# The second products of a gated layer written as seven products of sums

## The chip, the cores and the metric

The kernel runs on one core of one Trainium2 chip. The time is the device time of one execution in microseconds; each kernel is judged by the median of several executions. A profile is one further execution, recorded by the hardware profiler. The engines are named as in the profile: PE multiplies matrices (PEld is its loading of the stationary operand), DVE is VectorE, ACT is ScalarE, POOL is GpSimd, and SP only issues transfers.

## The reference

Two layers, each an attention part and a gated part, act on 2048 tokens of 448 features, in float32:

```
x = x + attention(layernorm(x), wqkv, wo)      # 16 heads of 28
x = x + gated(layernorm(x))
gated(y): g = y @ w_gate; u = y @ w_up         # 448 -> 1792
          h = sigmoid(g) * u
          return h @ w_down                    # 1792 -> 448
```

The change concerns `h @ w_down`, the second product of the gated part, in both layers.

## The kernel before

**Precision.** Every operand of a product is held as two float16 parts, high and low. A product is three matmuls: high by high, high by low, low by high.

**The gated part.** The tokens go in four blocks (`b`) of 512; the 1792 inner features go in seven pairs (`p`) of two chunks of 128, `p` and `p + 7`. For each block and pair, in this order:

- `gate_and_up` makes 512 tokens by 256 features of both g and u. It already has the form of seven products of sums in the place of eight, with 256 moving columns each: 78 matmuls (L512, in `of_halves`). Partial results leave the PSUM banks `chain` by copies of ACT (L1338) and the banks `side` by additions of DVE (L1354, L1361). ACT takes the sigmoid (L1365), DVE multiplies (L1368), and the result h, in two tiles `one` and `two`, is split by `split` into high (ACT, L205) and low (DVE, L206).
- `down` (L1295) multiplies h by its rows of `w_down`. It is called one pair late: the products of pair `p` stand on PE behind `gate_and_up` of pair `p + 1`. It is 24 matmuls with 448 moving columns (L1307 to L1309), adding up over the seven pairs of a block in four banks. At the block's end DVE adds the four banks to the residual `x` (L1312).

Between the pairs a list `steps` is worked off: the normalisation, the transfer out and back that turns it, and the sums and splits of the next block's operands (`half_steps`), on DVE, ACT and POOL.

**Order.** The order is the program's own (`manual_schedule`): each engine takes its instructions in the order written, and waits where an operand or a buffer isn't ready.

**Weights.** They are split once, during the attention of the first layer, by `Prepare` (DVE sums and splits, POOL's queue for its transfers), and lie in DRAM as `gu_parts` and `dn_parts`. In the gated part all of w_down's parts are resident (`dn`, four tiles), and three of the seven pairs of gate and up weights. The other four pairs share two places: `WeightsGated.used` (L1264) reloads them on POOL's queue. A pair's gate and up weights are two tiles of 800 KB. All large tiles come from 19 equal slots, handed out in the order in which they came free.

**Attention.** The exponential of the scores is taken by ACT, three units of 128 by 512 in one instruction (L1065); some units are computed by DVE instead (`score_aside`). The digits of the string `FEW` say how many for each head of the first layer.

Of the kernel before, what the change touches and what calls it, by code (L numbers as in the profile page):

```python
# [19 lines left out]
P = 128  # L20
# [20 lines left out]
PS = 2.0 ** -13  # L41
UNIT = 32768.0
# [9 lines left out]
AFTER = (None, 4, 5, None, 1, 2, None)  # L52

# [4 lines left out]
N_SUMS = 25  # L58
SHORT = ((10, 23, 12), (11, 24, 13), (8, 22, 9))
# [4 lines left out]
FEW = "2221121212121233"  # L64
# [41 lines left out]
def interleaved_layers(ctx: ExitStack, tc: tile.TileContext, x_in, wqkv, wo, w_gate, w_up,  # L106
# [143 lines left out]
    class Block:  # L250
# [87 lines left out]
        def steps(self):  # L338
            return [self.norm, self.squares,
                    lambda: (self.store((nc.sync, nc.scalar)), self.gather()),  # L340
                    lambda: None, lambda: None] + (
                        self.half_steps() if self.halves else
                        [lambda: self.ready(0, 1), lambda: self.ready(2, 3)])

# [186 lines left out]
    dn_parts = dpool.tile([4, P, 4, 2, D], F16, name="dn_parts")  # L531
# [323 lines left out]
    class Prepare:  # L855


        def __init__(self):
            nc.vector.memset(sums[:, 3:7], 0.0)
            self.part = cpool.tile([P, 2], F32, name="part", tag="part", bufs=1)  # L860
            self.raws, self.packs = big.ring(2), big.ring(2)
            self.halves = None
            tiles = [("o", 0)] + [("d", j) for j in range(4)] + [("gu", j) for j in range(7)]
            order = [(self.measure, what) for what in tiles] + [
                (self.split, what) for what in tiles[:5] + [(w, p) for p in range(NP)
                                                            for w in ("g", "u")]]
            self.read(*tiles[0])
            self.steps = deque()
            at = 6
            for i, (do, what) in enumerate(order):  # L870
                then = order[i + 1][1] if i + 1 < len(order) else None
                self.steps.append((at, lambda do=do, what=what, then=then:
                                   self.step(do, what, then)))
                at += 4 if do == self.measure else 5 if what[0] in "od" else 10
# [14 lines left out]
        def read(self, kind, j):  # L889
            if kind in "gu" and len(kind) == 1:  # L890
                if self.halves is None:
                    self.halves = big.at(self.raws, "raws", [P, 2, 1024])
                self.next = self.halves[:, (kind == "u") * 1]
            else:
                self.next = big.at(self.raws, "raw", [P, 2048])
            if kind == "o":
                load_rows(self.view(self.next, kind), wo, 0, D, nc.gpsimd)
            elif kind == "gu":
                for i, w in enumerate((w_gate, w_up)):
                    load_rows(self.view(self.next, kind)[:, i], w, j * 2 * P, 2 * P, nc.gpsimd)  # L900
            elif kind in "gu":
# [16 lines left out]
        def view(self, t, kind):  # L918
            if kind == "gu":
                return t.rearrange("p (w s c) -> p w s c", w=2, s=4)  # L920
            if kind in "gu":
                return t[:, 0:1024].rearrange("p (s z n) -> p s z n", s=4, z=2)
            return t[:, 0:4 * D].rearrange("p (s n) -> p s n", s=4)

        def step(self, do, what, then):
# [5 lines left out]
            if what == ("g", 0):  # L931
# [34 lines left out]
        def sizes(self):  # L966
# [4 lines left out]
            both_back(2, 5, 6, 2.0 ** -23)  # L971
# [3 lines left out]
        def split(self, raw, kind, j):  # L975
# [22 lines left out]
            else:  # L998
                n = self.count(j)
                t = big.at(self.packs, "pack", [P, 4, 2, D], F16)  # L1000
                scaled_split(t[:, 0:n, 0], t[:, 0:n, 1], v[:, 0:n], 6, nc.vector)
                self.pack = (dn_parts[j][:, 0:n], t[:, 0:n])
# [19 lines left out]
    def attend(layer, values, heads, last_values, gate, keep):  # L1022
# [133 lines left out]
        def more(g):  # L1156
            if g >= groups:
                return
            for u in main[3 * g:3 * g + 3]:
                if u in side:  # L1160
                    begin.append(side[u])
                if u % (NT * NB) == 8:
# [6 lines left out]
                    elif h == H - 1:  # L1169
                        gate.load_out()  # L1170
                        gate.load_gu(0)
# [33 lines left out]
    def out_project(outs, gate):  # L1205
# [15 lines left out]
        gate.load_gu(1)  # L1221
        gate.load_dn()
        gate.load_gu(2)
# [24 lines left out]
    class WeightsGated:  # L1248
# [3 lines left out]
        def __init__(self):  # L1252
            self.gu, self.dn = {}, []
# [5 lines left out]
        def load_gu(self, p, queue=nc.sync):  # L1259
            self.gu[p] = [big.get("gu", [P, N_SUMS, P], F16) for _ in range(2)]  # L1260
            for m in range(2):
                queue.dma_start(self.gu[p][m], gu_parts[p, m])

        def used(self, b, p):  # L1264

            after = AFTER[p]
            if b == NB - 1 and (after is None or after < p):
                big.put(*self.gu.pop(p))
            elif after is not None:
                big.put(*self.gu.pop(p))  # L1270
                self.load_gu(after, nc.gpsimd)

        def load_dn(self):
            j = len(self.dn)
            n = min(4, NF - 4 * j)
            self.dn.append(big.get("dn", [P, 4, 2, D], F16))
            nc.sync.dma_start(self.dn[-1][:, 0:n], dn_parts[j][:, 0:n])

    def gated(layer, first, wt, before_next):
        last = layer == LAYERS - 1  # L1280
        gu, dn = wt.gu, wt.dn
        wt.load_dn()
        wt.load_gu(3)
        wt.load_dn()
        wt.load_gu(6)
        wt.load_dn()
# [4 lines left out]
        pend = []  # L1291
        accs = {}
        held = {j: min(4, NF - 4 * j) for j in range(4)}

        def down(b, p, a, hl):  # L1295


            begin, end = p == 0 and a == 0, p == NP - 1 and a == 1
            if begin:
                accs[b] = [bank(j, "dnp")[:, 0:D] for j in range(TB)]  # L1300
            for j in range(TB):
                f = p + NP * (j // 2 ^ a)
                dw = dn[f // 4][:, f % 4]
                c = j if a == 0 else (j + 2) % 4
                s = slice(c * P, (c + 1) * P)
                pm = accs[b][j]
                nc.tensor.matmul(pm, hl[:, 0, s], dw[:, 0, :], start=begin, stop=False)  # L1307
                nc.tensor.matmul(pm, hl[:, 0, s], dw[:, 1, :], start=False, stop=False)  # L1308
                nc.tensor.matmul(pm, hl[:, 1, s], dw[:, 0, :], start=False, stop=end)  # L1309
                if end:  # L1310
                    t = b * TB + j
                    nc.vector.scalar_tensor_tensor(x[:, t, :], pm, back[:, 2:3], x[:, t, :],  # L1312
                                                   op0=ALU.mult, op1=ALU.add)
                    if last:
                        nc.sync.dma_start(x_dst[:, t, :], x[:, t, :])
            qrt.put(hl)
            if b == NB - 1 and a == 1:
                for f in (p, p + NP):
                    held[f // 4] -= 1
                    if not held[f // 4]:  # L1320
                        big.put(dn[f // 4])

        def gate_and_up(blk, w):
# [9 lines left out]
            lo, hi = slice(0, W // 2), slice(W // 2, W)  # L1333
# [33 lines left out]
            def times(out, v):  # L1367
                nc.vector.scalar_tensor_tensor(out, v, PS, out, op0=ALU.mult, op1=ALU.mult)  # L1368

            first(0)  # L1370
            first(1)
            apart(0)
            second(0)
            second(1)
            apart(1)
            third(0)
            third(1)
            c11_c22(0)
            c11_c22(1)
            sigmoid(one[0], one[0])  # L1380
# [4 lines left out]
            times(two[0][:, hi], chain[1][:, lo])  # L1385
            c12(0)
# [3 lines left out]
            qrt.put(one[1], two[1])  # L1390
            hls = []
# [6 lines left out]

        for b, p in seq:
            if p == 0:  # L1400
# [3 lines left out]
                elif not last:  # L1404
# [3 lines left out]
                    steps.extend([after[1].norm, after[1].squares, after[1].store,  # L1408
                                  after[1].gather])
            hls = gate_and_up(blks[b], gu[p])  # L1410
            wt.used(b, p)
# [4 lines left out]
            pend = [(b, p, a, hls[a]) for a in range(2)]  # L1416
            for f in (2 * p, 2 * p + 1):
                if 2 <= f:
                    run_fill(steps)
                if b == NB - 1 and not last:  # L1420
                    before_next(f)
        for d in pend:
            down(*d)
        return after if not last else None

# [39 lines left out]
    for layer in range(LAYERS):  # L1465
# [6 lines left out]
        def before_next(f, wq=wq):  # L1472
            if f == 6:
# [31 lines left out]
```

## Time and profile before

| | |
|---|---|
| median of three runs | 1931.62 us (1931.43 to 1933.78) |
| profiled execution | 1932.95 us, span 1930.8 us |
| PE busy in the span | 1915.8 us, 23392 matmuls |
| ACT, DVE, POOL busy | 1314.0, 1248.2, 164.5 us |
| first attention, from 120 us to 573.5 us | ACT busy 447.07 us with L1065 |
| gated part of layer 0, 607 to 976 us | PE busy 368.70 us, DVE 201.83, ACT 150.78 |
| gated part of layer 1, 1561 to 1927 us | PE busy 365.70 us, DVE 183.72, ACT 146.65 |
| granted PE clock | full in every slice |

The matmuls are pipelined: the record of one is longer than its share of the time. What a matmul costs in a stream is read from the distance between the starts of consecutive ones, not from its recorded duration.

### The profile page before, as it was taken

How to read it: one execution, taken by the hardware profiler on the slowest of the kernel's cores; microseconds unless marked ns; L12 is line 12 of the kernel's file. 1: busy time of each engine (PE TensorE's matmuls, PEld its weight loads, DVE VectorE, ACT ScalarE, POOL GpSimd, SP SyncE). 2: the span in 40 equal slices, each digit the busy share in tenths (PEclk: the TensorE clock that was granted, in tenths of full speed). 3: DMA queues.
4: the chain of work that ended last, by engine and by line, in shares of the span. 5: the costliest groups of instructions: out<-in, count | busy, mean ns of one | idle time of the engine just before them, and what ended most of it. 6: DMA issues, size and time to landing. Idle time of an engine off the chain costs nothing. (4 is left out here: it accounts for less than half of the span.)

```text
span 1930.8 us, 53585 instructions
## 1 busy us (share of the span) xinstructions
PE 1915.8 (99%) x23392; PEld 1327.5 (69%) x23392; DVE 1248.2 (65%) x2348; ACT 1314.0 (68%) x1574; POOL 164.5 (9%) x308
## 2 busy tenths in 40 slices
PE   8999999999999999999999999999999999999999
PEld 4455555555566777777744568799898777777776
DVE  6638878778676555555574487787778664655543
ACT  5569999999983344444345799999999544343432
POOL 2013322221001000000000000000000000000000
PEclk9999999999999999999999999999999999999999
DMA  5566664334216313232334321122111243333310
GB/s 172 158 197 176 187 195 129 107 102 113 64 62 242 107 69 108 81 128 79 101 111 131 94 51 47 30 51 51 42 36 65 104 169 117 107 111 97 115 49 20
DMA packets 90533, 201.49 MB, mean 104 GB/s; under 512 B 10830, under 2 KB 58030, under 8 KB 90160
## 3 DMA queue, kind: packets, MB, share of 16 engines
q1 hardware_dynamic: 65680, 111.02, 19.7%
q0 software_dynamic: 17776, 83.51, 13.0%
q8 instruction: 185, 3.03, 0.7%
q10 hardware_dynamic: 6832, 3.44, 0.7%
q14 instruction: 60, 0.49, 0.1%
HBM read 142.61 MB, written 47.98 MB: 99 GB/s over the span
## 5 line engine op out<-in xcount | busy, mean ns | idle before, releaser
L1065 ACT ACTIVATE prob_s<-sc 128x1536 f32<-128x1536 f32 x658 | 890.8, 1490 | 8.6 <-PE sc L1050 6.0
L1101 PE MATMUL acc<-prob_s,val_s 128*32 128x256 f32 (+3 forms) x7732 | 591.6, 383 | 0.0
L1050 PE MATMUL sc<-qp_s 114*32 114x512 f16 x7888 | 575.8, 379 | 0.9 <-ACT prob_s L1065 0.9
L512 PEld LDWEIGHTS <-gu_s 128*128 128x128 f16 x4368 | 427.3, 98 | 60.7 <-issue 1.3
L1050 PEld LDWEIGHTS <-qp_s 114*32 114x32 f16 x8192 | 315.8, 95 | 173.0 <-issue 80.0
L1101 PEld LDWEIGHTS acc<-prob_s,val_s 128*32 128x32 f32 x7732 | 321.5, 110 | 96.2 <-issue 7.0
L1354 DVE TENSOR_TENSOR one_q<-side,one_q 128x512 f32<-128x512 f32 x112 | 71.9, 683 | 298.0 <-PE side L512 298.0
L512 PE MATMUL chain<-xwide_s,gu_s 128*128 128x256 f16 x2016 | 247.5, 273 | 0.6 <-ACT one_q L1338 0.5
L1338 ACT COPY one_q<-chain 128x256 f32<-128x256 f32 x224 | 83.0, 372 | 205.5 <-PE chain L512 201.6
L1081 DVE SCALAR_TENSOR_TENSOR power_q<-power_q,expo_q 128x512 f32<-128x512 f32 x228 | 157.8, 692 | 7.8
L1307 PE MATMUL dnp<-dn_s,hhl_q 128*128 128x448 f16 x448 | 157.9, 352 | 0.0
L1308 PE MATMUL dnp<-dn_s,hhl_q 128*128 128x448 f16 x448 | 157.9, 352 | 0.0
L1309 PE MATMUL dnp<-dn_s,hhl_q 128*128 128x448 f16 x448 | 157.9, 352 | 0.0
L512 PE MATMUL side<-xshort_s,gu_s 128*128 128x256 f16 x1120 | 140.9, 272 | 0.0
L497 PE MATMUL qkp<-xhl_s,wqk_s 128*128 128x512 f16 x616 | 139.8, 383 | 0.4 <-ACT xhl_s L466 0.3
L497 PEld LDWEIGHTS <-wqk_s 128*128 128x128 f16 x616 | 60.6, 99 | 71.5 <-issue 2.7
L1130 DVE STREAM_TRANSPOSE oturned_q<-acc 128x512 f32<-128x512 f32 x32 | 22.9, 716 | 130.9 <-PE acc L1101 130.8
L512 PE MATMUL side<-xwide_s,gu_s 128*128 128x256 f16 x672 | 91.7, 273 | 0.0
L1101 PE MATMUL acc<-power_q,val_s 128*32 128x128 f32 (+3 forms) x284 | 88.6, 394 | 0.0
L1338 ACT COPY two_q<-chain 128x256 f32<-128x256 f32 x112 | 41.7, 372 | 67.4 <-PE chain L512 67.4
L1365 ACT ACTIVATE one_q<-one_q 128x512 f32<-128x512 f32 x56 | 35.3, 630 | 59.5 <-DVE one_q L1354 59.5
L1075 DVE TENSOR_SCALAR expo_q<-aside,base 128x512 f32<-128x512 f32 x76 | 56.8, 748 | 28.7 <-PE aside L1050 28.4
(188 smaller groups left out, 2080.0 us busy)
## 6 DMA issues: line engine op xcount, KB each, us to landing
gu_s<-gu_parts POOLq DMA_DIRECT2D x56, 800.0 KB, 4.9
qp_s<-qk_scr SPq DMA_DIRECT2D x96, 224.0 KB
gu_s<-gu_parts SPq DMA_DIRECT2D x20, 800.0 KB
qk_scr<-qkhl_q SPq DMA_DIRECT2D x56, 256.0 KB
gu_parts<-pack_s POOLq DMA_DIRECT2D x14, 800.0 KB, 3.9
xraw_s<-xt_scr SPq DMA_DIRECT2D x12, 768.0 KB
xt_scr<-xs_s SPq DMA_DIRECT2D x34, 224.0 KB
qp_s<-qk_scr SPq DMA_DIRECT2D x64, 112.0 KB
```

The costliest lines, as they stand in the source:

```text
L497: nc.tensor.matmul(pm, w, x, start=(i == 0), stop=(i == len(terms) - 1))
L512: nc.tensor.matmul(pm, a, x, start=(first and i == 0), stop=(i == len(terms) - 1), skip_group_check=True)
L1050: nc.tensor.matmul(ps[32 * j:32 * j + 32, :], hd.k[:, keys], hd.q[:, qb * W:(qb + 1) * W], start=True, stop=True, tile_position=(0, 32 * j))
L1065: nc.scalar.activation(prob[:, 0:n, :], ps[:, 0:n, :], AF.Exp, scale=exp_scale)
L1075: nc.vector.tensor_scalar(y, ps, base2[:, 0:1], -126.0, op0=ALU.mult, op1=ALU.max)
L1081: nc.vector.scalar_tensor_tensor(p, p, c[k], y, op0=ALU.add, op1=ALU.mult)
L1101: nc.tensor.matmul(acc[qb * VC:(qb + 1) * VC, s], v[:, kc % TB, h, :], probs[c * NB + qb][:, s], start=(kc == 0 and a == 0), stop=(kc == N ...
L1307: nc.tensor.matmul(pm, hl[:, 0, s], dw[:, 0, :], start=begin, stop=False)
L1308: nc.tensor.matmul(pm, hl[:, 0, s], dw[:, 1, :], start=False, stop=False)
L1309: nc.tensor.matmul(pm, hl[:, 1, s], dw[:, 0, :], start=False, stop=end)
L1338: nc.scalar.copy(to, pm)
L1354: nc.vector.tensor_tensor(one[m], side[m], one[m], op=ALU.add)
```

## The change

`w_down` is quartered for each pair: two chunks of features by two halves of 224 columns. h of a block is quartered too: two halves of 256 tokens by the two chunks. The eight products of quarters become seven products of sums (Winograd's form). Each is 256 tokens by 128 features by 224 columns, so six matmuls of 224 moving columns for a pair, 42 for a pair's seven products.

- **Weights.** `Prepare` makes seven steps `w` instead of four `d`: four subtractions of DVE and the high and low parts of seven (eight for the first three pairs) quarters or sums, in `dn_parts` with product as first index.
- **h.** Where `split` cast 512 columns twice and subtracted twice, `Operands` makes four sums of 256 columns on DVE, seven high parts of 256 on ACT and seven low parts of 256 on DVE. They are kept in a `store` of seven slots until the next block.
- **Order on PE.** Product `k` of block `b - 1`, over all its pairs, runs inside pair `p = k` of block `b`, in six places between the groups of `gate_and_up` (`along(0)` to `along(5)`). The first three pairs of block 0 (`USUAL`) keep eight products as 24 matmuls of 448 columns, one pair late as before. The last block's seven products stand by themselves at the end.
- **Sums in PSUM.** Products share banks 0 or 3, 1, and 2; after each product DVE adds a bank (or half of it) to its quarter of `x`: seven additions a block instead of four.
- **Residence.** Gate and up weights are now loaded for every pair, two pairs deep; w_down's parts are loaded product by product, three deep, on POOL's queue. The usual pairs' parts are loaded in `out_project` on SP's.
- **First attention.** `FEW` goes from 28 to 25 units on DVE. Steps of `Prepare` stand closer (7 instead of 10 places for a gate or up step).
- The next block's `steps` run in the places named by `portions`, two in a pair in most pairs.

```diff
-FEW = "2221121212121233"
+FEW = "2221212111111133"
+TAIL = (0, 1, 3, 2, 5, 4, 6)
...
+                s12, s34 = [qrt.get("sums", [P, 2, DN]) for _ in range(2)]
+                b11, b12, b21, b22 = [v[:, z, c:c + DN] for z in (1, 0) for c in (0, DN)]
+                for to, a, b in ((s12[:, 0], b12, b11), (s12[:, 1], b22, s12[:, 0]),
+                                 (s34[:, 0], b22, b12), (s34[:, 1], b21, s12[:, 1])):
+                    nc.vector.tensor_tensor(to, a, b, op=ALU.subtract)
...
+        def used_gu(self):
+            big.put(*self.gu.popleft())
+            if self.pairs:
+                self.load_gu(nc.gpsimd)
+
+        def used_dn(self):
+            big.put(self.dn.popleft())
+            if self.products:
+                self.load_dn(nc.gpsimd)
...
+            def high(self, ks, v):
+                for to, a in places(self.b, self.p, ks, v):
+                    nc.scalar.copy(to[:, :, 0], a)
+
+            def low(self, ks, v):
+                for to, a in places(self.b, self.p, ks, v):
+                    nc.vector.tensor_tensor(to[:, :, 1], a, to[:, :, 0], op=ALU.subtract)
+
+            def early(self):
+
+                self.s12, self.s34 = [qrt.get("hsums", [P, 2, W // 2]) for _ in range(2)]
+                a11, a22, a21 = self.one[:, 0], self.one[:, 1], self.two[:, 0]
+                self.high((0, 6), self.one)
+                for to, a, c, op in ((self.s12[:, 0], a21, a22, ALU.add),
+                                     (self.s12[:, 1], self.s12[:, 0], a11, ALU.subtract),
+                                     (self.s34[:, 0], a11, a21, ALU.subtract)):
+                    nc.vector.tensor_tensor(to, a, c, op=op)
+                self.high((1, 2), self.s12)
+
+            def late(self):
+                nc.vector.tensor_tensor(self.s34[:, 1], self.two[:, 1], self.s12[:, 1],
+                                        op=ALU.subtract)
+
+            def parts(self):
+                self.high((4, 5), self.s34)
+                self.high((3,), self.two[:, 1:2])
+                self.low((0, 6), self.one)
+                self.low((1, 2), self.s12)
+
+            def rest(self):
+                self.low((4, 5), self.s34)
+                self.low((3,), self.two[:, 1:2])
+                qrt.put(*self.tiles, self.s12, self.s34)
...
+        def piece(b, k, p, w, j, i, begin):
+
+            a = place(b, p, k)
+            pm = banks_of[i][:, j * DN:(j + 1) * DN]
+            t = slice(j * P, (j + 1) * P)
+            for n, (x, y) in enumerate(((0, 0), (0, 1), (1, 0))):
+                nc.tensor.matmul(pm, a[:, x, t], w[:, p, y], start=(begin and j == n == 0),
+                                 stop=(n == 2), skip_group_check=True)
...
+            if b > 0:
+                some = [q for q in (0, 1, 6, 2, 3, 4, 5) if q in of_block(b - 1)]
+                for q in some:
+                    i = {0: 0, 1: 1, 6: 2, 2: 3, 3: 4}.get(q, 5)
+                    at[i].append(lambda q=q, begin=(q == some[0]): pieces(
+                        b - 1, p, [q], wt.dn[0], begin))
...
+        b = NB - 1
+        w = list(wt.dn)
+        made.parts()
+        made.rest()
+        finish(*done)
+        for n in range(3):
+            pieces(b, TAIL[n], range(NP - 1), w[n], True)
+        for n in range(3):
+            pieces(b, TAIL[n], [NP - 1], w[n])
+            wt.used_dn()
+            finish(b, TAIL[n])
+        for k in TAIL[3:]:
+            if k == 6:
+                banks_of[0] = bank(0, "dnp")
+                for j in range(2):
+                    for p in range(NP):
+                        piece(b, k, p, wt.dn[0], j, 0, p == 0)
+                    add(b, 0, 0, 0, (j,))
+                    if last:
+                        t = b * TB + j
+                        nc.sync.dma_start(x_dst[:, t, :], x[:, t, :])
...
```

More of the change, by code (lines that the diff above doesn't have):

```diff
@@ L1252, in __init__ @@
         def __init__(self):
[L1253 removed]
+            self.gu, self.dn = deque(), deque()
+            self.pairs = deque(p for b in range(NB) for p in range(NP))
+            self.products = deque(list(range(NP)) * (NB - 1) + list(TAIL))
         def load_out(self):
@@ L1290, in gated, with place, places @@
         steps = deque()
[L1291 to L1298, printed above, removed]
-            if begin:
-                accs[b] = [bank(j, "dnp")[:, 0:D] for j in range(TB)]
+        banks_of = {}
+        def place(b, p, k):
+            return store[p][:, k] if b % 2 == 1 else store[k][:, p]
+        def places(b, p, ks, v):
+            if b % 2 == 1:
+                yield store[p][:, ks[0]:ks[-1] + 1:max(ks[-1] - ks[0], 1)], v
+            else:
+                for i, k in enumerate(ks):
+                    yield store[k][:, p:p + 1], v[:, i:i + 1]
@@ new lines, in pieces, with add @@
+        def pieces(b, k, pairs, w, begin=False):
+            i = bank_of(b, k)
+            begin = begin and k in (0, 1, 3)
+            if begin:
+                banks_of[i] = bank(i, "dnp")
+            for n, p in enumerate(pairs):
+                for j in range(2):
+                    piece(b, k, p, w, j, i, begin and n == 0)
+        def add(b, i, t, c, js=(0, 1)):
+            a, e = b * TB + 2 * t + js[0], b * TB + 2 * t + js[-1] + 1
+            v = x[:, a:e, c * DN:(c + 1) * DN]
+            pm = banks_of[i][:, js[0] * DN:(js[-1] + 1) * DN].rearrange("p (t n) -> p t n", n=DN)
+            nc.vector.scalar_tensor_tensor(v, pm, back[:, 2:3], v, op0=ALU.mult, op1=ALU.add)
@@ new lines, in leave, with finish, down @@
+        def leave(b, t):
+            if last:
+                for j in range(b * TB + 2 * t, b * TB + 2 * t + 2):
+                    nc.sync.dma_start(x_dst[:, j, :], x[:, j, :])
+        def finish(b, k):
+            add(b, bank_of(b, k), *HALVES[k])
+            if k == 5:
+                leave(b, 1)
+            if k == 6:
+                leave(b, 0)
+        accs = []
+        def down(p, a, hl):
+            begin, end = p == 0 and a == 0, p == USUAL - 1 and a == 1
+            if begin:
+                accs.extend(bank(j, "dnp")[:, 0:D].rearrange("p (c n) -> p c n", c=2)
+                            for j in range(TB))
@@ L1309, in down @@
[L1309 to L1315, printed above, removed]
-            qrt.put(hl)
[L1317 to L1321, printed above, removed]
@@ L1385, in gate_and_up @@
             times(two[0][:, hi], chain[1][:, lo])
+            along(4)
+            made = operands(one[0], two[0]) if operands else None
+            if made:
+                made.early()
             c12(0)
```

205 lines of the change are left out of this document (142 added, 63 removed).

## The prediction

> **What bounds the kernel now.** I read the page first, then the order of time on PE in the gated part, then what other engines wait for. From the page:
>
> ```profile
> span 1930.8 us, 53585 instructions
> PE 1915.8 (99%) x23392; PEld 1327.5 (69%) x23392; DVE 1248.2 (65%) x2348; ACT 1314.0 (68%) x1574; POOL 164.5 (9%) x308
> ...
> L1065 ACT ACTIVATE prob_s<-sc 128x1536 f32<-128x1536 f32 x658 | 890.8, 1490 | 8.6 <-PE sc L1050 6.0
> ```
>
> PE is busy throughout, but a busy PE only says that records touch. The timeline of PE tells more: starts that follow at a fixed distance are a full stream. Its columns are start and duration in us.
>
> ```profile
> 1577.86 0.35 PE L1307 MATMUL dnp<-dn_s,hhl_q 128*128 128x448 f16 x1
> ...
> 1582.39 1.47 PE L512 MATMUL chain<-xwide_s,gu_s 128*128 128x256 f16 x12
> 1583.70 0.82 PE L512 MATMUL side<-xwide_s,gu_s 128*128 128x256 f16 x6
> ...
> 1909.29 1.47 PE L512 MATMUL chain<-xwide_s,gu_s 128*128 128x256 f16 x12
> ...
> 1917.80 0.35 PE L1307 MATMUL dnp<-dn_s,hhl_q 128*128 128x448 f16 x1
> ```
>
> ```profile
> 976.19 9.66 PE L497 MATMUL qkp<-xhl_s,wqk_s 128*128 128x512 f16 x44
> ...
> L497 PE MATMUL qkp<-xhl_s,wqk_s 128*128 128x512 f16 x616 | 139.8, 383 | 0.4 <-ACT xhl_s L466 0.3
> ```
>
> A pair's 24 products of `down` take 1582.39 - 1577.86 = 4.53 us, 188.8 ns each for 448 columns. Its 78 matmuls of gate and up take 1917.80 - 1909.29 = 8.51 us, 109.1 ns each for 256 columns (12 in 1583.70 - 1582.39 = 1.31 us). For 512 columns, 44 records less the tail of the last give (9.66 - 0.383) / 43 = 215.7 ns. The three lie on one line: (215.7 - 188.8) / 64 = 0.42 and (188.8 - 109.1) / 192 = 0.415 ns a column. So the gated part is bound by PE's columns, 13.04 us a pair, and other engines wait for PE:
>
> ```profile
> DVE one_q L1354 <- PE side L512: 158.1, 25, 8.0
> ...
> PE chain L512 <- ACT one_q L1338: 0.2, 1, 0.2
> ```
>
> These are the waits of layer 1's gated part: DVE waited 158.1 us for PE, PE 0.2 us for ACT.
>
> **The change, part by part.**
>
> *Products (both layers).* Before: 2 x 28 x 24 = 1344 matmuls, x 188.8 ns = 253.7 us. After: three pairs of each layer keep 24, so 144 x 188.8 ns = 27.2 us; 25 pairs have 42 of 224 columns, so 2100. No row has 224 columns. The line gives 109.1 - 32 x 0.415 = 95.8 ns; the nearest row, 256 columns, bounds it above at 109.1. I take 95.8 and 201.2 us, because three widths lie on the line. Change: 27.2 + 201.2 - 253.7 = **-25.3 us**; with 109.1 it would be +2.6. A full pair goes from 13.04 to 8.51 + 42 x 0.0958 = 12.53 us.
>
> What could hold narrow matmuls above the line is the loading of weights. The rows of PEld by shape, mean ns behind the busy time, and the one run of narrow matmuls:
>
> ```profile
> L512 PEld LDWEIGHTS <-gu_s 128*128 128x128 f16 x4368 | 427.3, 98 | 60.7 <-issue 1.3
> ...
> L1050 PEld LDWEIGHTS <-qp_s 114*32 114x32 f16 x8192 | 315.8, 95 | 173.0 <-issue 80.0
> ...
> L448 PEld LDWEIGHTS turn<-ident,xn_s 128*128 128x128 f32 x48 | 6.0, 149 | 4.6 <-DVE xn_s L283 4.0
> ```
>
> ```profile
> 1545.97 1.91 PE L448 MATMUL turn<-ident,xn_s 128*128 128x128 f32 x16
> 1547.72 0.35 PE L522 MATMUL op<-wout_s,ot_s 128*128 128x448 f16 x1
> ```
>
> A float16 load shows 98 ns, which is over 95.8. But float32 loads of 149 ns followed each other every (1547.72 - 1545.97) / 16 = 109 ns, so a recorded load overlaps the next by some 40 ns; and 32 columns show 95 ns where 128 show 98, so most of it is a delay that a stream needn't pay.
>
> The Trainium skill, "TensorE: Matmul & The Clock Gate", section "LDWEIGHTS (loading the stationary operand)", gives a load 1/1.2 ns for each column, 106.7 ns for 128, which speaks against this change: by it the 2100 would cost 224.1 us and the gain would be 2.4. The same page's section "Weight-path perf modes" says that 128 float16 weights load faster; the float32 transposes agree with the first figure, the float16 rows with the second, and no run here has a float16 matmul narrow enough to decide.
>
> *VectorE and ScalarE in the gated part.* Spacing on DVE and its busy time:
>
> ```profile
> 1627.79 1.29 DVE L1354 TENSOR_TENSOR one_q<-side,one_q 128x512 f32<-128x512 f32 x2 [5.48 <-PE side L512]
> ...
> 1630.12 0.75 DVE L1361 TENSOR_TENSOR two_q<-side,two_q 128x256 f32<-128x256 f32 x2
> ...
> L1354 DVE TENSOR_TENSOR one_q<-side,one_q 128x512 f32<-128x512 f32 x56 | 36.0, 683 | 158.1 <-PE side L512 158.1
> L1361 DVE TENSOR_TENSOR two_q<-side,two_q 128x256 f32<-128x256 f32 x56 | 20.9, 415 | 0.0
> ...
> L1312 DVE SCALAR_TENSOR_TENSOR x<-dnp,back,x 128x448 f32<-128x448 f32 x16 | 9.8, 677 | 6.4 <-PE dnp L1309 6.4
> ...
> 1561.00:1927.00 366.00, 365.70 (x2851) 278.59 (x2848) 183.72 (x371) 146.65 (x348) 20.85 (x39) 1.00 0.27 92
> ```
>
> Back to back, 512 columns cost 1.29 - 0.68 = 0.61 us, 256 cost 0.75 - 0.415 = 0.335. The last row holds PE, PEld, DVE, ACT and POOL in order: DVE has 183.72 / 28 = 6.6 us a pair, ACT 5.2. DVE gains four sums (1.34), its low parts go from 2 x 0.61 to 7 x 0.335 = 2.35 or, in odd blocks, 3 x 0.61 + 0.335 = 2.17 (+1.1 at most), and additions go from four to seven a block (+0.3): 9.3 us. ACT gains three copies of 256, about 1 us: 6.2. PE's pair is 8.51 + 24 x 0.0958 = 10.81 us in block 1 (four pairs' products) and 12.53 in blocks 2 and 3, so this hides behind PE. In block 0, pairs 4, 5 and 6 have 8.51 us, and there the next block's work (some 2 us) is done by pair 4.
>
> *Pairs without cover.* Between pairs 4, 5, 6 of block 0 and the first of block 1 no products of `down` stand any more; PE goes straight on. The trace has such a place, the first two pairs:
>
> ```profile
> 1560.20 1.47 PE L512 MATMUL chain<-xwide_s,gu_s 128*128 128x256 f16 x12
> 1561.51 0.82 PE L512 MATMUL side<-xwide_s,gu_s 128*128 128x256 f16 x6
> 1562.58 1.47 PE L512 MATMUL chain<-xwide_s,gu_s 128*128 128x256 f16 x12 [0.24 <-ACT one_q L1338]
> ...
> 1569.12 1.15 PE L512 MATMUL chain<-xwide_s,gu_s 128*128 128x256 f16 x9
> ```
>
> They take 8.92 us (1560.20 to 1569.12) and 8.74 (to 1577.86), 0.41 and 0.23 over 8.51. In the new order `early` puts three sums (1.0 us) and four copies ahead of the last sigmoid on DVE and ACT, and the next pair's copies (L1338), for which `second` waits on PE, queue behind that. Bounds 0.23 and 1.5 (that whole queue shown); nearer the row, I take 0.5: 3 x 2 x 0.5 = **+3.0 us** (1.4 to 9).
>
> *First attention.*
>
> ```profile
> 120.00:573.50 453.50, 447.07 (x332) 1.00 0.47 136
> ```
>
> ACT is busy 447.07 of 453.5 us with L1065, 1.347 each. 25 instead of 28 units on DVE leave 999 / 3 = 333 instructions in place of 332: **+1.35 us** (0 if PE hides it). `Prepare`'s sums and parts add work to DVE, off this chain; the three dropped units give most of it back, and POOL has little else queued there.
>
> *Transfers.* In blocks 1 to 3 a pair now needs two gate and up tiles and one of w_down, 2.4 MB on POOL's queue; behind it stand POOL's normalisation steps. Issue, rate by the microsecond (GB/s is the last column), and landing:
>
> ```profile
> 1617.11 1.07 POOL L1262 DMA_DIRECT2D gu_s<-gu_parts  x2 [25.83 <-PE side L512]
> ...
> 1620.00:1621.00 1.00, 1.00 (x7) 0.52 (x6) 1.00 (x4) 0.53 (x1) 0.00 (x0) 1.00 1.06 442
> ...
> DMA to landing us min/median/max: 3.6/4.8/8.2
> ```
>
> At some 420 GB/s that is 5.8 us plus a start of 1.6 (the quickest landing, 3.6, less 0.82 MB / 420 GB/s), within the 10.8 or 12.5 us to the pair that needs it; in block 0 two tiles have 8.51. Cost zero, cover named. SP's twelve small loads in `out_project` replace larger ones; nothing urgent follows them.
>
> *Ends.* The last block's products stand alone, counted above; pair 6's parts (about 3 us) hide behind 108 matmuls (10.3 us).
>
> ```profile
> 974.69 2.46 DVE L1312 SCALAR_TENSOR_TENSOR x<-dnp,back,x 128x448 f32<-128x448 f32 x4 [5.00 <-PE dnp L1309]
> ```
>
> Before, the next layer's first product (976.19) used bank 0, which this addition had read already. Now bank 0 is the last read: a matmul's tail plus a 224-column addition, **+0.7 us** once (0 to 1.1). At the kernel's end the last addition has half the columns of 677 ns: **-0.3**.
>
> **Sum.** -25.3 + 3.0 + 1.35 + 0.7 - 0.3 = -20.55. The profiled execution took 1932.95 us, 2.15 beyond its span; 1912.4 follows, and since it lay 1.3 above the median, **1911** for the median.
>
> **Rivals.**
>
> *The load of weights sets the pace.* Place: each of the 2100 narrow matmuls. For it: 98 ns recorded, and 109 in the float32 run. Against: the overlap. At 98 ns +4.6 us, 1916; at 109.1 +27.9, **1939, slower**. It decides above 95.8 + 20.55 / 2.1 = 105.6 ns. The Trainium skill's 106.7 ns lies just beyond that.
>
> *DVE and ACT come late in the short pairs.* For: 9.3 us of DVE against 8.51 and 10.81, and pair 1 of block 1 gets eight instructions of squares and transposes at once. Against: DVE's 158.1 us of waiting. If the three short pairs and the seven of block 1 lose 0.4 us more each, 2 x 10 x 0.4 = 8: **1919**.
>
> *Weights come late.* At the end the fourth product's load is written only 12 matmuls (1.15 us) ahead of its use; a landing of 3.6 to 8.2 us would cost 2.5 to 7 a layer, some 9 in all: **1920**. Against: slots go out oldest first, so its slot came free long before and POOL can issue early.
>
> **How the numbers follow.** Forecast 0.60; loads of weights 0.16 (faster 0.05, same 0.03, slower 0.08); late engines 0.13 (0.03 of it slower: 1 us lost in each of the twenty pairs); late weights 0.06 (0.02 slower); anything else 0.05, slower by 0.04. Within 0.2% is 3.9 us either side, about what measurement can tell from no change. So faster 0.80, same 0.03, slower 0.17. The forecast's own bounds are 1906 (no waits) to 1918; the range, with most of the middle of the rivals, 1904 to 1932, leaves out the slow ends.
>
> **What would show it.** Starts of the new matmuls 95.8 ns apart in the stretch at a layer's end, or 98 to 109 by the first rival. 12.5 us between pairs of blocks 2 and 3. Little PE idle ahead of L512's chain in block 0, put down to ACT. 333 instructions of L1065 in the first attention. No wait of PE for DMA. It is wrong if the narrow spacing is above 100 ns, or PE waits over 1 us in pairs of block 1.

## The result, and the profile after

Before and after were timed by turns on one chip: 1932.61 us before (seven runs, 1931.43 to 1933.78) and 1927.46 us after (seven runs, 1923.98 to 1928.66). The ratio is 0.997, with an interval of 0.9960 to 0.9979: faster, by about 5 us. The forecast was 1911, some 20 us faster. The direction held, three quarters of the gain is missing.

The page of the kernel after, its head and the rows that answer to those of before:

```profile
span 1926.6 us, 56295 instructions
PE 1898.3 (99%) x24316; PEld 1342.7 (70%) x24316; DVE 1409.8 (73%) x2802; ACT 1368.5 (71%) x1741; POOL 229.1 (12%) x433
...
L1095 ACT ACTIVATE prob_s<-sc 128x1536 f32<-128x1536 f32 x659 | 892.2, 1485 | 9.3 <-PE sc L1080 6.1
...
L1403 PE MATMUL dnp<-dn_s,hparts_s 128*128 128x224 f16 x2100 | 235.8, 259 | 1.1 <-DVE x L1420 1.1
...
L1403 PEld LDWEIGHTS <-hparts_s 128*128 128x128 f16 x2100 | 202.1, 98 | 6.2 <-issue 1.4
...
L521 PE MATMUL side<-xshort_s,gu_s 128*128 128x256 f16 x1120 | 142.8, 275 | 11.5 <-DVE one_q L1491 11.3
```

PE's busy time fell by 17.5 us, the span by 4.2, with the granted clock full in nearly all of it. The last row is the one to follow: ahead of the matmuls of `side`, a part of gate and up, PE stood idle for 11.5 us, nearly all of it for one line of DVE. The view of waits says how it is spread (total us, times, longest):

```profile
DVE t_q L372 <- DMA xraw_s<-xt_scr: 19.7, 4, 9.9
...
PE side L521 <- DVE one_q L1491: 11.3, 6, 4.3
```

Six waits of PE, the longest 4.3 us; and DVE itself waited 19.7 us for a transfer, up to 9.9 at a time. The timeline of layer 1's gated part puts the two side by side. The columns are start and duration; the bracket holds the idle time before, and what ended it:

```profile
1574.59 0.86 SPq L317 DMA_DIRECT2D xt_scr<-xs_s  x2
1574.85 0.54 POOL L1294 DMA_DIRECT2D gu_s<-gu_parts  x1 [6.21 <-DVE xs_s L305]
...
1576.84 0.54 POOL L1294 DMA_DIRECT2D gu_s<-gu_parts  x1 [1.45 <-PE side L521]
...
1577.24 1.57 ACTq L317 DMA_DIRECT2D xt_scr<-xs_s  x2
...
1580.11 0.69 DVE L211 TENSOR_TENSOR hhl_q<-two_q,hhl_q 128x512 f16<-128x512 f32 x1
...
1580.92 1.47 PE L521 MATMUL chain<-xwide_s,gu_s 128*128 128x256 f16 x12
...
1585.44 0.39 SPq L325 DMA_DIRECT2D xraw_s<-xt_scr  x1
...
1587.25 1.26 PE L521 MATMUL chain<-xshort_s,gu_s 128*128 128x256 f16 x10
1590.71 0.76 DVE L372 TENSOR_TENSOR t_q<-xraw_s 128x256 f32<-128x256 f32 x2 [9.92 <-DMA xraw_s<-xt_scr]
...
1592.06 1.28 DVE L1491 TENSOR_TENSOR one_q<-side,one_q 128x512 f32<-128x512 f32 x2
1592.80 2.18 PE L521 MATMUL side<-xshort_s,gu_s 128*128 128x256 f16 x10 [4.29 <-DVE one_q L1491]
...
1600.10 1.47 PE L521 MATMUL chain<-xwide_s,gu_s 128*128 128x256 f16 x12
```

Read it from the bottom. Pair 2 of block 0 takes 1600.10 - 1580.92 = 19.18 us, where 13.04 was its cost. In the middle PE waits 4.29 us for DVE's addition L1491, which empties the PSUM banks that PE wants to fill again. DVE reaches it only at 1592.06, because from 1580.80 on (the end of L211) it stands before L372, the first sum of the *next* block, whose tile is still on its way through DRAM. The tile's store was issued at 1574.59, the gather that reads it back at 1585.44, and the sum could begin at 1590.71, 16.1 us after the store. DVE had come to that sum 6.2 us behind the store. Beside the store POOL had issued two loads of gate and up weights, at 1574.85 and 1576.84.

The trip is no new one. In the kernel before, the timeline has the same store, gather and sum:

```profile
1589.34 0.86 SPq L312 DMA_DIRECT2D xt_scr<-xs_s  x2
...
1598.77 0.39 SPq L320 DMA_DIRECT2D xraw_s<-xt_scr  x1
...
1606.63 0.75 DVE L363 TENSOR_TENSOR t_q<-xraw_s 128x256 f32<-128x256 f32 x2
```

There the sum began 17.3 us after the store, and found its tile: no bracket. So the change shortened the distance between the store and DVE's coming to the sum from 17.3 us to 6.2.

The wait costs more than itself, as the table by stretch shows (PE, PEld, DVE, ACT and POOL busy, granted clock, DMA share, GB/s):

```profile
1588.00:1592.00 4.00, 0.50 (x5) 0.30 (x4) 1.29 (x4) 0.71 (x2) 0.00 (x0) 1.00 0.40 149
...
1593.00:1594.00 1.00, 1.00 (x7) 0.67 (x6) 0.83 (x2) 0.75 (x2) 0.00 (x0) 0.50 0.00 0
1594.00:1595.00 1.00, 1.00 (x6) 0.66 (x5) 0.87 (x3) 0.10 (x1) 0.54 (x1) 0.50 0.00 0
1595.00:1596.00 1.00, 1.00 (x4) 0.40 (x3) 0.88 (x3) 1.00 (x3) 0.00 (x0) 0.50 0.63 77
1596.00:1597.00 1.00, 1.00 (x6) 0.48 (x5) 1.00 (x3) 0.86 (x2) 0.00 (x0) 0.82 0.70 269
```

After the idle time the clock is granted at 0.50 for over 3 us. Of the pair's 6.14 us too many, 4.29 are the wait. From the matmul behind the wait (1592.80) to the next pair (1600.10) PE takes 7.30 us for what costs 1.09 + 4.53 = 5.62 in a full stream, so 1.68 go to the slow clock; the 0.17 left is the tail of the last record before the wait, which is longer than its share of the time. In layer 0 the same pair takes 18.45 us, 5.41 too many.

Two more waits are on the timeline, in pair 1 of block 1 and at the end:

```profile
1660.18 0.65 DVE L305 STREAM_TRANSPOSE xs_s<-xn_s 128x448 f32<-128x448 f32 x1
1660.75 1.25 DVE L1491 TENSOR_TENSOR one_q<-side,one_q 128x512 f32<-128x512 f32 x2
...
1661.46 1.30 PE L521 MATMUL side<-xshort_s,gu_s 128*128 128x256 f16 x10 [1.29 <-DVE one_q L1491]
...
1892.23 27.48 PE L1403 MATMUL dnp<-dn_s,hparts_s 128*128 128x224 f16 x285
...
1920.25 2.17 PE L1403 MATMUL dnp<-dn_s,hparts_s 128*128 128x224 f16 x21 [0.54 <-DVE x L1420]
```

L305 is the last of eight scalings and transposes that stand ahead of L1491 on DVE: PE waits 1.29 us. At the end, the last product's second half waits 0.54 us for the addition that reads its first half. The row of 285 gives the price of a narrow matmul: (27.48 - 0.26) / 284 = 95.85 ns.

### The profile page after: what moved, and what is told of

Its sections match the earlier page's. It is cut to its first block, busy times and chain, and to the rows that moved or that the text cites. A ratio compares the mean times of both kernels' runs of the same rounds, so it can differ in the third digit from the quotient of the medians.

```text
span 1926.6 us, 56295 instructions
## 1 busy us (share of the span) xinstructions
PE 1898.3 (99%) x24316; PEld 1342.7 (70%) x24316; DVE 1409.8 (73%) x2802; ACT 1368.5 (71%) x1741; POOL 229.1 (12%) x433
## 5 line engine op out<-in xcount | busy, mean ns | idle before, releaser
L1131 PE MATMUL acc<-prob_s,val_s 128*32 128x256 f32 (+3 forms) x7766 | 574.9, 383 | 0.1
L1080 PE MATMUL sc<-qp_s 114*32 114x512 f16 x7900 | 559.4, 379 | 0.9 <-ACT prob_s L1095 0.9
L521 PEld LDWEIGHTS <-gu_s 128*128 128x128 f16 x4368 | 427.5, 98 | 63.7 <-issue 16.3
L1080 PEld LDWEIGHTS <-qp_s 114*32 114x32 f16 x8192 | 277.1, 95 | 206.5 <-issue 96.5
L1131 PEld LDWEIGHTS acc<-prob_s,val_s 128*32 128x32 f32 x7766 | 283.0, 110 | 135.0 <-issue 11.2
L1403 PE MATMUL dnp<-dn_s,hparts_s 128*128 128x224 f16 x2100 | 235.8, 259 | 1.1 <-DVE x L1420 1.1
L1403 PEld LDWEIGHTS <-hparts_s 128*128 128x128 f16 x2100 | 202.1, 98 | 6.2 <-issue 1.4
L521 PE MATMUL side<-xshort_s,gu_s 128*128 128x256 f16 x1120 | 142.8, 275 | 11.5 <-DVE one_q L1491 11.3
L1491 DVE TENSOR_TENSOR one_q<-side,one_q 128x512 f32<-128x512 f32 x112 | 71.7, 681 | 54.0 <-PE side L521 51.8
L1294 POOL DMA_DIRECT2D gu_s<-gu_parts x104 | 55.7, 536 | 398.8 <-PE side L521 233.1
L1356 ACT CAST hparts_s<-hsums_q 128x256 f16<-128x256 f32 (+1 forms) x144 | 68.9, 489 | 28.4 <-DVE hsums_q L1370 20.9
L682 ACT ACTIVATE qkhl_q<-qkp 128x512 f16<-128x512 f32 x56 | 33.2, 594 | 75.9 <-PE qkp L506 74.3
L1131 PE MATMUL acc<-power_q,val_s 128*32 128x256 f32 (+3 forms) x274 | 85.1, 393 | 0.0
```

Of the source, the lines that this page charges most:

```text
L521: nc.tensor.matmul(pm, a, x, start=(first and i == 0), stop=(i == len(terms) - 1), skip_group_check=True)
L1080: nc.tensor.matmul(ps[32 * j:32 * j + 32, :], hd.k[:, keys], hd.q[:, qb * W:(qb + 1) * W], start=True, stop=True, tile_position=(0, 32 * j))
L1131: nc.tensor.matmul(acc[qb * VC:(qb + 1) * VC, s], v[:, kc % TB, h, :], probs[c * NB + qb][:, s], start=(kc == 0 and a == 0), stop=(kc == N ...
L1294: queue.dma_start(self.gu[-1][m], gu_parts[p, m])
L1356: nc.scalar.copy(to[:, :, 0], a)
L1403: nc.tensor.matmul(pm, a[:, x, t], w[:, p, y], start=(begin and j == n == 0), stop=(n == 2), skip_group_check=True)
```

## The experiments

Each edit is one to the kernel after. `portions` says, for a block and pair, how many of the next block's `steps` are taken at each of six places between the matmul groups; steps taken at the last place stand behind the pair's own additions. The theory: DVE's queue is in order, and a sum of the next block stands at its head before its tile is back, so the additions behind it come late and PE stops. The rivals: DVE simply has too much to do in block 0; and, as to why the tile is late, either the store was too late or the weight loads on POOL's queue share the DMA engines with it.

**e1_late: the sum that waits goes behind the pair's additions.**

```diff
-            return ((0, 1, 1, 0, 0, 0), (0, 1, 1, 0, 0, 1), (0, 2, 1, 0, 0, 1),
+            return ((0, 1, 1, 0, 0, 0), (0, 1, 1, 0, 0, 1), (0, 1, 1, 0, 0, 2),
```

> Edit: in block 0 the first sum of the next block's operands (r11, which reads the transposed tile that comes back from DRAM) is taken from the place before c11_c22 of pair 2 to the place after its c12. Theory (DVE's queue is held by r11, which waits 9.9 us for the transfer, and the c11_c22 additions that PE needs stand behind it): no PE idle of over 1 us in pair 2, the granted clock stays at 1.00 there, pair 2 with the products behind it takes 13.1 to 13.5 us instead of 19.2 and 18.5, and the median falls by 10 to 12 us, to about 1916. Rival (DVE simply has too much work in block 0): the same microseconds turn up in pairs 3 to 6, and the median falls by 3 at most, to about 1924.

Measured: 1917.24 us (1915.19 to 1918.12), beside 1932.07 for the kernel before, ratio 0.9921 (0.9905 to 0.9938). Its timeline:

```profile
1575.39 1.47 PE L521 MATMUL chain<-xwide_s,gu_s 128*128 128x256 f16 x12
...
1581.45 1.29 DVE L1491 TENSOR_TENSOR one_q<-side,one_q 128x512 f32<-128x512 f32 x2 [6.17 <-PE side L521]
...
1585.03 0.75 DVE L372 TENSOR_TENSOR t_q<-xraw_s 128x256 f32<-128x256 f32 x2
...
1588.45 1.47 PE L521 MATMUL chain<-xwide_s,gu_s 128*128 128x256 f16 x12
```

Pair 2 takes 13.06 us. DVE does the same work, and now waits for PE (6.17); pairs 3 to 6 of layer 1 take 13.37, 8.51, 8.86 and 8.86 us, as in the kernel after. So DVE isn't too full, and that rival falls. One step's place was worth 1926.6 - 1915.0 = 11.6 us of span.

**e2_early: the squares in pair 0, so that the store goes out earlier; the sum stays where it was.**

```diff
-            return ((0, 1, 1, 0, 0, 0), (0, 1, 1, 0, 0, 1), (0, 2, 1, 0, 0, 1),
+            return ((0, 1, 1, 0, 0, 2), (0, 1, 0, 0, 0, 0), (0, 2, 1, 0, 0, 1),
```

> Edit: r11 stays where it is; instead the squares of block 1 move from pair 1 to the end of pair 0, so that the transfer out and back starts some 5 us earlier. Theory: r11's wait for the transfer falls from 9.9 us to about 5, which the time between c11_c22 and c12 nearly covers; PE idle in pair 2 falls from 4.3 us to under 1, the median by 8 to 11 us. Rival (the transfer is slow because the gate and up weights share the engines with it): started earlier it meets the loads issued at the end of pair 0, lands less than 2 us earlier, and the median falls by under 5 us.

Measured: 1926.73 us (1922.81 to 1928.82), ratio 0.9968 (0.9956 to 0.9979): no gain over the kernel after, as the rival in its expectation had it.

```profile
1573.40 0.86 SPq L317 DMA_DIRECT2D xt_scr<-xs_s  x2
1573.41 0.93 ACTq L317 DMA_DIRECT2D xt_scr<-xs_s  x2
...
1580.01 0.39 SPq L325 DMA_DIRECT2D xraw_s<-xt_scr  x1
...
1589.67 0.76 DVE L372 TENSOR_TENSOR t_q<-xraw_s 128x256 f32<-128x256 f32 x2 [9.85 <-DMA xraw_s<-xt_scr]
...
1591.76 2.29 PE L521 MATMUL side<-xshort_s,gu_s 128*128 128x256 f16 x10 [2.65 <-DVE one_q L1491]
```

The store went out 1.2 us earlier on SP and 3.8 on ACT, the gather 5.4, but the tile was there only 1.0 us earlier, 16.3 us after the store (the gated part itself began 0.2 us later here). What the transfer was given at its start it lost on the way: ahead of the gather POOL had issued three weight loads, at 1574.02 and 1577.44, and the gather took 9.7 us, against 5.3 in the kernel after. PE's wait is still there (2.65 and, in layer 0, 3.88). Pair 2 takes 17.29 us in layer 1, 1.9 less than in the kernel after, but 19.75 in layer 0, 1.3 more: there the clock stayed at 0.50 for some 6.8 us (642.4 to 649.2) behind the wait.

**e7_reuse: no weight loads beside the store.** The loads for pairs 2 and 3 of block 0, four tiles of 800 KB, are left out, and these pairs use again the gate and up weights of pairs 0 and 1. The result is therefore not the layer's, but the work on PE, DVE and ACT is the same. The sum stays in its early place.

```diff
+            if len(self.pairs) > NB * NP - 4:
+                self.gu.append(self.gu.popleft())
+                self.pairs.popleft()
+                return
             big.put(*self.gu.popleft())
```

> Edit to the changed kernel: pairs 2 and 3 of block 0 use the gate and up weights of pairs 0 and 1 once more, so that the four tiles of 800 KB issued at the ends of pairs 0 and 1 are not loaded; everything else stays, r11 at its place before c11_c22. (The result of these two pairs is another one; the work on every engine is the same.) Theory now, after the earlier start of the transfer brought nothing: the transfer out and back is slow because these loads share the transfer engines with it. Then the tile lands 4 us or more earlier than in the changed kernel (16 us after the first store was issued), r11 waits under 6 us instead of 9.9, and PE's idle in pair 2 falls from 4 us to under 1. Rival (the transfer is slow by itself, by its two steps and its short rows): it lands at the same distance and PE idles 3.5 to 4.3 us as before.

Measured: 1918.17 us in a single execution, span 1916.5; the fastest of the seven of the kernel after took 1923.98.

```profile
1570.33 0.85 SPq L317 DMA_DIRECT2D xt_scr<-xs_s  x2
...
1576.59 0.39 SPq L325 DMA_DIRECT2D xraw_s<-xt_scr  x1
...
1577.06 0.59 POOL L1294 DMA_DIRECT2D gu_s<-gu_parts  x1 [16.52 <-DMA xt_scr<-xs_s]
...
1581.14 0.76 DVE L372 TENSOR_TENSOR t_q<-xraw_s 128x256 f32<-128x256 f32 x2 [5.31 <-DMA xraw_s<-xt_scr]
```

Store to gather takes 6.3 us instead of 10.85, store to sum 10.8 instead of 16.1. One load, for pair 4, still goes out 0.5 us behind the gather, so the trip isn't quite alone. DVE still waits 5.31 us for the tile, but PE doesn't: it has that much in hand, and pair 2 takes 13.24 us. So the loads that are left out, on POOL's queue, where the change put loads for every pair, had lengthened the trip by 5.3 us. The Trainium skill, "DMA: Bandwidth & Descriptors", section "Queues, rings and completion order", says that each DMA engine goes round between the queues that have work, a packet at a time; a trip that gets longer beside another queue's loads agrees with it. Either remedy alone, the sum's place (e1) or fewer loads beside the trip (e7), takes PE's wait away.

**e3_spread: the two squares steps of pairs 0 and 1 of block 1 behind the additions.**

```diff
-        return (0, 1, 1, 0, 0, 0)
+        return (0, 1, 0, 0, 0, 1) if b == 1 and p < 2 else (0, 1, 1, 0, 0, 0)
```

> Edit: in pairs 0 and 1 of block 1 the second half of the normalisation and of the squares goes from the place before c11_c22 to the place after c12. Theory (the four scalings and transposes stand on DVE ahead of the c11_c22 additions): the wait of PE for DVE in pair 1 of block 1 (1.3 us in each layer) and in pair 0 (0.35) goes; those two pairs together take 1.5 us less in each layer, 3 us in all. Rival (DVE is full over the whole of block 1): the wait moves to pairs 2 and 3 and block 1 is as long as before.

Measured: 1934.79 us in a single execution, where the slowest of the kernel after's seven took 1928.66. The waits in pairs 0 and 1 were gone; but the transpose came later, and with it the store, and now the first sum of block 2 met its tile too early:

```profile
1667.97 0.84 SPq L317 DMA_DIRECT2D xt_scr<-xs_s  x2
...
1685.81 0.76 DVE L372 TENSOR_TENSOR t_q<-xraw_s 128x256 f32<-128x256 f32 x2 [5.34 <-DMA xraw_s<-xt_scr]
...
1687.89 1.96 PE L521 MATMUL side<-xshort_s,gu_s 128*128 128x256 f16 x10 [2.75 <-DVE one_q L1491]
```

The trip took 17.8 us here. (PE waited 1.23 us for ACT, too, in the pair ahead.) This is the mechanism of block 0, made in another place by moving only the work ahead of it.

**e5_banks: the last product's two halves in banks of their own (2 and 1, both were in 0).**

```diff
...
-                banks_of[0] = bank(0, "dnp")
                 for j in range(2):
+                    i = 2 - j
+                    banks_of[i] = bank(i, "dnp")
                     for p in range(NP):
-                        piece(b, k, p, wt.dn[0], j, 0, p == 0)
-                    add(b, 0, 0, 0, (j,))
+                        piece(b, k, p, wt.dn[0], j, i, p == 0, True)
+                    add(b, i, 0, 0, (j,))
...
```

> Edit: the two halves of the last product are added up in banks 2 and 1 instead of both in bank 0. Theory (PE's first matmul of the second half waits for the addition that reads the first half out of the same bank): the wait of 0.54 us before the last 21 matmuls goes in both layers, and so does that of 0.54 us before the first product of the next layer's projection; 1.6 us in all. Rival (PE waits for something else that DVE does): the waits stay.

Measured: 1925.94 us in a single execution, inside the kernel after's range, so that the time alone shows nothing; the waits do. From 1900 us on, the products run to the end without a break, in one row of PE's timeline:

```profile
1899.80 20.19 PE L1403 MATMUL dnp<-dn_s,hparts_s 128*128 128x224 f16 x209
```

The 0.54 us at the end of each layer, and the 0.54 before the next layer's first product, are gone: 1.6 of the 2.4 us by which the span is shorter (1924.2 after 1926.6). So the matmul's wait went by the bank and not by the bytes: the addition reads the columns of the first half, the matmul writes those of the second. Each bank is one tile of the program, so no run here shows whether the chip alone would have asked for the wait. The Trainium skill, "PSUM — Partial Sum Buffer", section "PSUM bank collisions raise a hardware error ⚠️", says that two engines must be kept apart in one bank and partition quadrant even where their columns differ; the wait of 0.54 us is what keeping apart costs here.

**e8_both: e1, e5, and another order for block 1.**

```diff
+        if b == 1:
+            return ((0, 1, 1, 0, 0, 0), (0, 1, 0, 0, 0, 0), (0, 1, 0, 0, 0, 1),
+                    (0, 2, 0, 0, 0, 0), (0, 0, 0, 0, 0, 2), (0, 1, 1, 0, 0, 1),
+                    (0, 1, 1, 0, 0, 0))[p]
```

> Edit to the changed kernel: r11 of block 0 behind c12 (as in the late run), the last product in two banks, and in block 1 only one half of the squares ahead of c11_c22 in each of pairs 1 and 2, the transfer after pair 2, and its first sums after c12 of pair 4, so that no sum waits for it. Theory: against the run with r11 alone (1917) the two waits of 1.3 us in pair 1 of block 1 and three of 0.54 us go: 4 us, to 1913. Rival (DVE is full in block 1): the waits come back in pairs 2 to 6, and the gain is the 1.6 us of the banks.

Measured: 1917.41 us (1916.85 to 1919.9), ratio 0.9921 (0.9907 to 0.9935): as e1, nothing gained. The wait of 1.29 us was gone, but others came, of which this is the clearest:

```profile
1668.35 0.53 POOL L1294 DMA_DIRECT2D gu_s<-gu_parts  x1 [8.40 <-DMA xt_scr<-xs_s]
...
1675.61 0.83 PE L521 MATMUL chain<-xwide_s,gu_s 128*128 128x256 f16 x6 [0.64 <-DMA gu_s<-gu_parts]
```

On POOL a weight load now stood behind a step that waited for the store, was issued 8.4 us late, and PE waited for weights. Three more waits of PE for ACT (0.25, 0.46 and 1.37 us) came behind it.

**e9_late_few: e1, with the first attention's division of before, 28 units on DVE.**

```diff
-FEW = "2221212111111133"
+FEW = "2221121212121233"
```

> Edit to the changed kernel: r11 of block 0 behind c12, and the digits of FEW as before the change, 28 units of the first attention on DVE instead of 25. Theory (ScalarE's instructions set the length of the first attention): one instruction fewer on ACT, the gated part of layer 0 starts 1.3 us earlier than with r11 alone (610.7 us), and the median is 1916. Rival (DVE, with the denser steps of the weights' preparation, comes late with its units): the first attention is as long or longer, the start at 611 us or later.

Measured: 1915.54 us (1915.15 to 1917.16), ratio 0.9914 (0.9899 to 0.9930); the gated part of layer 0 began at 608.81 us where e1's began at 610.68. That is 1.9 us for one instruction of 1.35 on ACT. But among the seven profiles with 25 units this start lies anywhere from 609.08 to 612.05, and with 28 units at 608.57 in e10 and 610.36 in e11. The ranges overlap, and so do the times of e1 and e9: that 28 units are faster is likely, but not shown.

**e10_three: e9 with the banks of e5.**

> Three edits to the changed kernel together: r11 of block 0 behind c12, 28 units of the first attention on DVE, the last product in two banks. If the gains add up (11 + 1.7 + 1.6 us below the changed kernel's 1927.5), the median is 1914. If the 0.54 us waits only hid something else, it is that of the run without the banks, 1915.5.

Measured: 1912.47 us (1911.60 to 1913.15), beside 1932.56 for the kernel before, ratio 0.9894 (0.9878 to 0.9911), somewhat below the expected sum of 1914. It has the lowest median of all, 20.1 us below before, and, beside the 0.24 us behind the first pair that before has too, these two waits of PE are left in a gated part:

```profile
692.83 1.31 PE L521 MATMUL side<-xshort_s,gu_s 128*128 128x256 f16 x10 [0.35 <-DVE one_q L1491]
...
705.16 1.30 PE L521 MATMUL side<-xshort_s,gu_s 128*128 128x256 f16 x10 [1.29 <-DVE one_q L1491]
```

**e11_four: e10, and half of the squares of block 1's pair 1 one place later.**

```diff
-        return (0, 1, 1, 0, 0, 0)
+        return (0, 1, 0, 1, 0, 0) if b == 1 and p == 1 else (0, 1, 1, 0, 0, 0)
```

> As the run before, and in pair 1 of block 1 the second half of the squares stands behind the c11_c22 additions on DVE instead of ahead of them, without moving the transfer. Theory (only the place in DVE's order counts, if no sum is made to wait for a transfer): PE's wait of 1.3 us there falls under 0.4, and the next pair loses 0.3 us at most at its second product; 1 us less in each layer, 1912. Rival (any delay of DVE in that pair comes back in the next): no gain, 1914.

Measured: 1912.84 us (1912.39 to 1913.72), ratio 0.9896 (0.9879 to 0.9912): as e10. The wait of 1.29 became one of 0.77, a pair later, so most of the delay came back, as the rival in its expectation had it:

```profile
1650.72 0.81 PE L521 MATMUL side<-xwide_s,gu_s 128*128 128x256 f16 x6 [0.77 <-DVE two_q L1498]
```

A gated part is 0.45 us shorter than in e10, which its median doesn't show.

## Why the prediction was right in part, and where it failed

By its own steps, from the profiles (before 1932.95 us, after 1928.41):

| Step | Forecast, us | Found, us |
|---|---|---|
| *Products* | -25.3 | -25.3: 95.85 ns each, where 95.8 was read off the line |
| *Pairs without cover* | +3.0 | +3.6: layer 1's pairs take 8.51, 8.86, 8.86 and 11.73, 1.6 over; layer 0's 2.0 |
| *First attention* | +1.35 | +1.5 (gated part begins at 610.81, before at 609.34), 659 instructions for 658 |
| *Ends* | +0.7 - 0.3 | +2.0: three times 0.54 at banks, and 0.4 more after the last product |
| *Transfers* | 0 | +11.55 in pair 2 of block 0 (6.14 and 5.41) |
| pair 3 of block 0 (not in the sum) | 0 | +0.66 (0.33 in each layer; it stays in e1 and e7, so it isn't the transfer's) |
| pair 1 of block 1 (a rival, not in the sum) | 0 | +3.0 (1.5 in each layer) |
| Sum | -20.55 | -3.0; measured -4.5 |

What is left over, 1.5 us, lies mostly in the gated parts, 0.6 a layer: in the kernel before, four pairs of layer 0 and three of layer 1 took 13.22 or 13.23 us, 0.18 over their cost, and in the later blocks of the kernel after no pair is over.

**The step that failed** is "*Transfers.*" with its "Cost zero, cover named". It asked whether the weights reach their pair in time, and they do: no wait of PE for a DMA is in the profile after. It did not ask whom their transfers meet. The next block's tile goes to DRAM and back on SP's and ACT's queues at the same moment, and its trip took 16.1 us with the loads and 10.8 with four of them left out (e7). The root is in the paragraph on *VectorE and ScalarE*, where it says "there the next block's work (some 2 us) is done by pair 4": the next block's sums were counted as DVE's time. Their place, at the head of an in-order queue 6.2 us behind the store, was not priced as a wait, though the places are named in the kernel after (`portions`) and the old distance, 17.3 us, is in the trace of before. With that place changed (e1) pair 2 takes 13.05 and 13.06 us in the two layers, and the span falls by 11.6 us, against the table's 11.55.

**The rivals.** *The load of weights sets the pace* is refuted: 2100 loads show 98 ns, and the stream runs at 95.85. The 106.7 ns for 128 columns that is worked out from the Trainium skill's rule ("TensorE: Matmul & The Clock Gate", section "LDWEIGHTS (loading the stationary operand)"), an estimate, doesn't bind these float16 loads; the measurement decides. *DVE and ACT come late in the short pairs* was half right: the eight instructions at once in pair 1 of block 1 do stop PE, for 1.5 us a pair, but it is that pair and not ten. PE's wait of 1.29 us there is also what the prediction named as a sign of being wrong, over 1 us in a pair of block 1; it cost 3.0 us, a quarter of what pair 2 of block 0 did. *Weights come late*, at the end, doesn't appear. The case that came true, a transfer that comes late for DVE, was none of them.

**The number.** 1911 was near what the new form is worth: e10, with the same products, a better place for one sum, other banks and the old division of the first attention, takes 1912.47. Its last two edits recover terms that the forecast had charged, and the wait in block 1 stays in it, so the nearness is partly luck: two errors that cancel. It is luck, too, that the range, 1904 to 1932, holds the result: it reached that far for rivals of another kind.

## What to carry to other kernels

Moving a consumer of a transfer earlier is a change of that transfer's deadline: measure from the trace how long the trip takes (16 us here for a store and a gather), and compare it with the distance between producer and consumer in the new order, on an engine that takes its instructions in order. An instruction that waits at the head of such a queue stops everything behind it, and what stands behind may be PE's only way to a free PSUM bank. New loads on a queue that has room are not free: look for the small, urgent transfer that shares the DMA engines with them.

## What the runs showed of the hardware

- A short stop of PE costs a second time. After 4.29 us idle the clock was granted at 0.50 for over 3 us. In e2 an idle time of 2.65 us did the same, and in e3 one of 2.75; after 1.29 us the granted clock stayed full, and the next ten matmuls took 1.30 us, against 1.25 without a wait. How long the clock stays low does not follow the idle time: some 3.4 us behind 4.29, some 6.8 behind 3.88 (e2, layer 0). The view by stretch of e2's layer 1:

```profile
1591.00:1592.00 1.00, 0.24 (x2) 0.18 (x2) 1.00 (x3) 0.20 (x1) 0.00 (x0) 0.64 0.00 0
1592.00:1593.00 1.00, 1.00 (x7) 0.69 (x6) 0.83 (x2) 0.70 (x2) 0.00 (x0) 0.50 0.00 0
1593.00:1594.00 1.00, 1.00 (x6) 0.75 (x5) 0.82 (x3) 0.14 (x1) 0.54 (x1) 0.50 0.00 0
```

  The Trainium skill, "TensorE: Matmul & The Clock Gate", section "HAM oscillation — how this bites in real kernels", warns of idle gaps over about 3.4 us; here 2.65 us were enough.

- Float16 matmuls of 224 columns, each with its own load of 128 columns, run at 95.85 ns, on the straight line through 256, 448 and 512 columns (109.1, 188.8 and 215.7 ns), though each load shows 98 ns.

- An issue that SP made early gained little: the store and gather took 16.3 us when started 1.2 us sooner (e2), 16.1 in the kernel after, 17.8 for block 2's tile in e3, and 10.8 with no weight loads beside the store and one behind the gather (e7).
